# Local attention with a routed mixture of experts: 16-bit one-hot tables, slot lines by rounding, gate columns in one load, and a new order of work

## The chip, the cores and the metric

The kernel runs on one core of one Trainium2 chip. The metric is the device time of one execution in microseconds (us); the figure before the change is the median of three runs. An execution that was recorded by the hardware profiler gives the page and the rows below.

## What is computed

Causal attention in a window of 128 positions with a linear bias for each head (8 batches, 8 heads, 576 positions, 64 wide), and behind it a mixture of 8 experts with the two best for each of the 4608 tokens:

```python
scores = np.where(mask, scale * q @ k.T + bias, -1e9)       # 0 <= i - j < 128
x = (softmax(scores) @ v)  ->  (4608, 512)
noisy = x @ w_gate + np.log1p(np.exp(x @ w_noise)) * noise
top2 = the two largest of the 8 noisy logits; top2_w = softmax over the two
for e in range(8):
    h = np.maximum(x[mask_e] @ w1[e], 0.0)                  # 512 -> 1024
    out[mask_e] += top2_w * (h @ w2[e])                     # 1024 -> 512
```

## The kernel before, in words

**The order is made while the program is built.** Each piece of work is a strand, a Python generator that asks for an engine with a planned cost in us and a due time (its rank), for a buffer of a ring, or for an event. The class `Order` simulates the engines by those costs: each free engine takes the ready piece with the lowest rank, and in that order the instructions are written into each engine's queue. On the chip the queues are then worked off in that fixed order, each instruction waiting for its data. So a planned cost never changes an instruction, only the order. The constants at the top (`ZERO` to `LARGEST`) are offsets of due times and delays; `STAGE` has one for each step of an attention unit, `FFN0, FFN1` spread the due times of the first wave's products, `HOLD` holds the first two experts' weight loads until a planned time, `PACE` and `REST` space the later ones. `Order.cost` raised each VectorE cost by 3% once the planned time was past `FFN1`.

**Attention** goes in 32 pairs of heads (4 for each batch) by 5 units of 128 positions. A unit's scores are made on TensorE (`scores`, line 598), VectorE adds the bias and takes the row extremes (`top`, 604), ScalarE takes the exponential (`soft`, 612), TensorE turns it (`trans`, 619), ScalarE or VectorE copies it back (`evac`, 305), and `weigh` (636) multiplies with the values. The values carry 16 further columns with the products of values and gate weights, so that the same `weigh` brings the gate logits: `gates_of_values` multiplies the transposed values `vt` by `wgn` (525). `wgn` holds w_gate and w_noise at two column offsets, zero elsewhere; four loads fill it (`gate_weight`, 447) over a memset. All direct loads are issued by SyncE, in its own fixed order.

**Routing** of a batch (`route`) makes the noisy logits, the two best experts and each token's slot in its expert's list. A slot number is split into a line and a column of 64 (`halves`): by a shift and a mask on integers, with copies between types. Then two one-hot tables are made by comparing with a running number, for 10 = 5 x 2 (tile, choice) entries each: `hot[0]` by 80 (expert and line, 893) and `hot[1]` by 64 (column, 897). The second is multiplied by the token numbers (901, on GpSimd in six batches, on VectorE in two), and ten matmuls (`list_`, 905) sum the entries into 80 lines of 64, which GpSimd adds into the lists in memory. `next_lines` makes the lines from which the next batch goes on.

**The experts** run in two waves. The first takes experts 0 and 1 with the tokens that early batches gave (blocks of 256, 256, 256, 192), during attention and behind it: gathers, splitting of tokens and weights into two 16-bit parts, up products (1459), ReLU (1618, 1650), down products (1659), scatters that add into the output (1796). The second takes what is left of these and the six other experts, ranked by the length of their lists; their blocks of 512 tokens use a seven-product scheme (1496) whose sums of tokens, weights and quadrants are made on VectorE (1274, 1574 to 1611). VectorE also makes the low parts of the weights (1270, 1290) and of the tokens (1399). Expert 2's loads (1192) need the ranking, which needs the last batch's routing.

Of the kernel before, what the change touches and what calls it, by code (L numbers as in the profile page):

```python
# [29 lines left out]
LINE, SPAN = 64, 10  # L30
LINES = 88
# [16 lines left out]
ZERO = 2019.65  # L48
LOAD = 1075.19
VALUES = 1169.98  # L50
GATE = (413.12, 503.1)
GATES = -311.61
ROUTE = -79.16
SCATTER = (-1036.89, -486.7, 213.65)
FFN0, FFN1 = 288.77, 555.18
WEIGHTS = ((918.12, 272.55), (959.66, -236.26))
SEQUENCE = ((0, 0), (0, 1), (1, 0), (1, 1), (0, 2), (1, 2), (0, 3), (1, 3))
TOKENS = -394.6
STAGE = (538.41, 414.48, -338.92, -406.83, 42.73, -373.27, 193.47, -830.41)
# [60 lines left out]
class Order:  # L120
# [141 lines left out]
def attention_moe(ctx: ExitStack, tc: tile.TileContext, qk_, v, vt_, w_gate, w_noise, noise, w12,  # L262
# [83 lines left out]
    steps_ = const.tile([128, E * SPAN], F16, name="steps")  # L346
    numbers = const.tile([128, NQ], F32, name="numbers")
# [8 lines left out]
    lines_ = const.tile([128, 2, E], I32, name="lines")  # L356
# [31 lines left out]
    def set_ups():  # L388
# [9 lines left out]
        def counts_():  # L398
            for t, pattern, first_, step in ((steps_, [[1, E * SPAN]], 0, 0), (numbers, [[64, NQ]], 1, 1),
# [37 lines left out]
    def gate_weights():  # L437
        yield begun
        parts = Event(4)
        for z, w in enumerate((w_gate, w_noise)):  # L440
            for h in range(2):
                spawn(gate_weight(z, w, h, parts))
        yield parts
        mark(gated)

    def gate_weight(z, w, h, parts):
        yield from move(2e4, -LOAD + GATES, lambda: nc.sync.dma_start(
            wgn[h * D:h * D + D, :, h * 16 + z * E:h * 16 + z * E + E],
            dram(w, h * D * E, [[E, D], [128 * E, 4], [1, E]])))
        mark(parts)  # L450
# [275 lines left out]
    def divided(k, low, high, r7):  # L726
# [24 lines left out]
        yield dve(0.45, r7, sums)  # L751
        for o, i, c in halves_:
            to = xs_[y][:, i:NQ:2].rearrange("p i (h c) -> p i h c", h=4)[:, :, 2 * z:2 * z + 2]
            lt = lts[b][:, i:NQ:2, 2 * (k % NP):2 * (k % NP) + 2]
            yield dve(0.49 if c == 3 else 0.36, r7, lambda: times(o, i, c, to, 0, D))
            yield dve(0.2 if c == 3 else 0.17, r7, lambda: times(o, i, c, lt, D, D + 16))
# [77 lines left out]
    def route(b):  # L834
# [7 lines left out]
        yield act(0.09, rank, lambda: nc.scalar.activation(u, lg[:, :, 8:16], AF.Abs))  # L842
# [3 lines left out]
        yield act(0.1, rank, lambda: nc.scalar.activation(positive, lg[:, :, 8:16], AF.Relu), False)  # L846
# [42 lines left out]
        def tables(eng, z):  # L889

            if z == 0:
                shape = [128, 2 * NQ, E * SPAN]
                eng.tensor_tensor(hot[0], ef.rearrange("p i k -> p (i k)")[:, :, None].to_broadcast(shape),
                                  steps_[:, None, :].to_broadcast(shape), op=OP.is_equal)
            elif z == 1:
                shape = [128, 2 * NQ, LINE]
                eng.tensor_tensor(hot[1], d.rearrange("p i k -> p (i k)")[:, :, None].to_broadcast(shape),
                                  steps_[:, None, 0:LINE].to_broadcast(shape), op=OP.is_equal)
            else:
                h = hot[1].rearrange("p (i k) c -> p i (k c)", k=2)  # L900
                eng.tensor_tensor(h, h, numbers[:, :, None].to_broadcast([128, NQ, 2 * LINE]), op=OP.mult)
# [1165 lines left out]
```

## Time and profile before

| what | us |
|---|---|
| median of 3 runs | 1023.29 |
| their range | 1021.52 to 1024.88 |
| the profiled execution's own time | 1020.78 |
| its span, first to last instruction | 1018.9 |

The page gives each engine's busy time, a picture of the span in 40 slices, and the chain of work that ended last. In the rows below an engine is named PE (TensorE products), PEld (its weight loads), DVE (VectorE), ACT (ScalarE), POOL (GpSimd) or SPq (SyncE's queue, which issues loads), and L598 is line 598 of the kernel. The clock column (PEclk) is the granted clock of TensorE as a share of the higher of its two levels, 2.4 GHz; the lower is 1.2.

### The profile page before, as it was taken

How to read it: one execution, taken by the hardware profiler on the slowest of the kernel's cores; microseconds unless marked ns; L12 is line 12 of the kernel's file. 1: busy time of each engine (PE TensorE's matmuls, PEld its weight loads, DVE VectorE, ACT ScalarE, POOL GpSimd, SP SyncE). 2: the span in 40 equal slices, each digit the busy share in tenths (PEclk: the TensorE clock that was granted, in tenths of full speed). 3: DMA queues.
4: the chain of work that ended last, by engine and by line, in shares of the span. 5: the costliest groups of instructions: out<-in, count | busy, mean ns of one | idle time of the engine just before them, and what ended most of it. 6: DMA issues, size and time to landing. Idle time of an engine off the chain costs nothing.

```text
span 1018.9 us, 25787 instructions
## 1 busy us (share of the span) xinstructions
PE 979.8 (96%) x9734; PEld 701.8 (69%) x9734; DVE 796.2 (78%) x2733; ACT 564.3 (55%) x1367; POOL 331.0 (32%) x442
## 2 busy tenths in 40 slices
PE   7999999999899999979999999999999999999997
PEld 4776777776666689657668666856767686666774
DVE  6989989798997633987799598959978995998240
ACT  6977678485535424664567555634665655544221
POOL 1079432343834224321324142404331232321013
PEclk9999999999999999999999999999999999999999
DMA  8999999794149455895559474949693676638024
GB/s 315 410 312 318 312 336 328 236 295 73 42 93 243 76 81 90 162 218 134 94 109 217 104 130 91 226 74 171 97 236 59 151 147 166 108 65 127 4 40 52
DMA packets 175534, 166.59 MB, mean 164 GB/s; under 512 B 128928, under 2 KB 139248, under 8 KB 175408
## 3 DMA queue, kind: packets, MB, share of 16 engines
q1 hardware_dynamic: 157888, 125.59, 45.9%
q0 software_dynamic: 17520, 39.34, 21.8%
q8 instruction: 77, 1.26, 0.5%
q14 instruction: 49, 0.40, 0.1%
HBM read 95.11 MB, written 40.91 MB: 133 GB/s over the span
## 4 chain that ended last, share of the span: by engine, by line
PE 79%; DVE 13%; POOL 2%; DMA 2%; issue 2%; ACT 1%; SPq 0%; POOLq 0%; DVEq 0%; ACTq 0%
PE bank L1659 31%; PE bank L1496 18%; PE bank L1459 12%; PE bank L636 5%; PE bank L1664 4%; PE bank L598 3%; PE bank L619 3%; DVE bhl L1611 1%; DVE p L604 1%; DMA qk<-in_qk_dram 1%; DVE side L1599 1%; DVE held L1290 1%; POOL held L1287 1%; DVE x L748 1%; DVE pT L305 1%
## 5 line engine op out<-in xcount | busy, mean ns | idle before, releaser
L1659 PE MATMUL bank<-held,bhh 128*128 128x512 f16 x734 | 218.4, 379 | 2.6 <-ACT bhh L1618 2.6
L1496 PE MATMUL bank<-bx,held 128*128 128x256 f16 x1824 | 210.5, 273 | 6.8 <-ACT side L301 6.3
L1796 POOL DMA_INDIRECT out_dram<-yo,ix x58 | 96.0, 1655 | 338.0 <-ACT yo L301 281.6
L1496 PEld LDWEIGHTS <-held 128*128 128x128 f16 x1824 | 178.7, 98 | 33.2 <-issue 8.2
L1659 PE MATMUL bank<-held,bhl 128*128 128x512 f16 x367 | 139.1, 379 | 1.5 <-DVE bhl L1611 1.5
L1659 PEld LDWEIGHTS <-bhh 128*128 128x128 f16 x784 | 75.8, 98 | 88.9 <-ACT bhh L1618 4.1
L1459 PE MATMUL bank<-ax,held 128*128 128x256 f16 (+6 forms) x1380 | 133.9, 252 | 2.0 <-DVE ahl L1650 1.5
L1459 PEld LDWEIGHTS <-held 128*128 128x128 f16 x1380 | 115.8, 98 | 17.7 <-issue 3.8
L612 ACT ACTIVATE p<-p,nm 128x192 f32<-128x192 f32 (+2 forms) x288 | 103.7, 427 | 22.4 <-DVE nm L604 21.6
L301 ACT ACTIVATE xt<-xg,fit 128x512 f16<-128x512 f32 (+5 forms) x93 | 62.6, 677 | 60.3 <-DVE fit L1366 27.2
L1618 ACT ACTIVATE bhh<-side 128x512 f16<-128x512 f32 x69 | 42.4, 627 | 94.8 <-DVE side L1599 93.2
L604 DVE CUSTOM_DVE_ANT_0 p<-bank,bias 128x192 f32<-128x192 f32 (+2 forms) x288 | 81.8, 327 | 5.5 <-PE bank L598 4.8
L301 ACT ACTIVATE held<-held,wsc 128x512 f16<-128x512 f32 x93 | 63.3, 713 | 28.9 <-DVE held L1274 14.3
L636 PE MATMUL bank<-vraw,pT 64*64 64x81 f32 (+1 forms) x2048 | 76.7, 240 | 1.6 <-DVE pT L305 0.6
L636 PEld LDWEIGHTS bank<-vraw,pT 64*64 64x64 f32 (+1 forms) x2048 | 68.5, 137 | 10.2 <-issue 2.0
L1338 POOL DMA_INDIRECT xg<-xs_dram,ix x48 | 51.8, 1080 | 70.6 <-DVE xt L1399 36.8
L619 PE MATMUL bank<-ident,p 128*128 128x128 f32 x416 | 68.1, 286 | 6.3 <-ACT pT L301 2.8
L1659 PEld LDWEIGHTS <-bhl 128*128 128x128 f16 x392 | 38.3, 98 | 48.9 <-DVE bhl L1611 2.9
L598 PE MATMUL bank<-qk 64*64 64x192 f32 (+2 forms) x1152 | 65.7, 326 | 6.5 <-DMA qk<-in_qk_dram 5.1
L1290 DVE SCALAR_TENSOR_TENSOR held<-held,wsc,held 128x512 f16<-128x512 f32 x96 | 70.9, 767 | 0.0
L1204 ACT ACTIVATE junk<-held 128x512 bf16<-128x512 f32 x104 | 65.1, 626 | 6.2 <-DMA held<-in_w_dram 4.3
L619 PEld LDWEIGHTS bank<-ident,p 128*128 128x128 f32 x416 | 45.7, 142 | 32.3 <-ACT pT L301 7.6
(284 smaller groups left out, 1793.1 us busy)
## 6 DMA issues: line engine op xcount, KB each, us to landing
held<-in_w_dram SPq DMA_DIRECT2D x61, 512.0 KB
qk<-in_qk_dram SPq DMA_DIRECT2D x31, 576.0 KB
vraw<-in_v_dram SPq DMA_DIRECT2D x16, 810.0 KB
out_dram<-xg SPq DMA_DIRECT2D x10, 1024.0 KB
vt<-in_vt_dram SPq DMA_DIRECT2D x16, 576.0 KB
xs_dram<-x SPq DMA_DIRECT2D x16, 320.0 KB
xs_dram<-x SPq DMA_DIRECT2D x16, 256.0 KB
bx<-xt SPq DMA_TRANSPOSE x96
```

The lines of the kernel that those rows point to most:

```text
L301: nc.scalar.activation(o, i, AF.Copy, **kw)
L598: nc.tensor.matmul(s[j % 2][half:half + 64, o:o + c], qk[rows, j * 64:j * 64 + 64], qk[rows, k1 - c:k1], start=True, stop=True)
L604: nc.vector.tensor_tensor_reduce(out=p[:, place(j):place(j) + c], in0=s[z][:, o:o + c], in1=bias4[:, g, z, 192 - c:192], scale=-0.125, sca ...
L612: nc.scalar.activation(pv, pv, AF.Exp, bias=nm[:, z:z + 1], scale=-1.0)
L619: nc.tensor.transpose(t[:, z * 128:z * 128 + 128], p[:, a * 128:a * 128 + 128], ident)
L636: nc.tensor.matmul(o[z * 64:z * 64 + 64, c:c + VC], pt[rows, slot, from_:from_ + 64], t[rows, block, hh], start=(o is first_, z) not in be ...
L1204: nc.scalar.activation(junk, raws_flat(t, z), AF.Abs, accum_out=wam[:, e % 2, z, f:f + 1])
L1290: nc.vector.scalar_tensor_tensor(lo, t, sc, hi, op0=OP.mult, op1=OP.subtract)
L1459: nc.tensor.matmul(t[:, 0:blk.n], wp[:, c], blk.x[:, x + c, 0:blk.n], start=c == 0 and z == 0, stop=c == 3 and z == 2)
L1496: nc.tensor.matmul(t[:, a % 2 * HALF:a % 2 * HALF + HALF], wp, blk.x[:, x], start=first_, stop=False, skip_group_check=True)
L1659: nc.tensor.matmul(blk.y[j][0:r], h[:, cs], wp, start=f == 0 and m == 0, stop=f == 7 and m == 2)
L1796: ins = nc.gpsimd.indirect_dma_start(out=out, out_offset=bass.IndirectOffsetOnAxis(ap=blk.ix[0:r, j:j + 1], axis=0), in_=t[0:r, 0:DM], in_ ...
```

## The change

Four things are done at once. **Tables:** the running numbers become a tile of 80 x 10 in 16 bits, row and column of each entry are kept as 16-bit tiles of 10, and the tables are laid out with the 10 entries innermost; all operands of the comparisons and of the multiplication are then 16 bits wide. The ten matmuls read the tables with a step of 10 elements. **Slot lines:** the line is found by rounding in float (multiply, add, add and subtract a large constant) in place of the integer shift, mask and copies; `next_lines` does the same. **Gate columns:** the host lays w_gate and w_noise out as `wgn` holds them, zeros included; one load brings them, and four loads and a memset go. **Order:** most due times and delays and a number of planned costs are new, and the 3% on VectorE are gone. The diff, cut to its core; in the lines left out other planned costs change (steps of the route, copies and sums of attention), unused tiles go, and the new argument is passed on:

```diff
+WHOLE = 1.5 * 2.0 ** 23
...
-ZERO = 2019.65
-LOAD = 1075.19
-VALUES = 1169.98
-GATE = (413.12, 503.1)
-GATES = -311.61
-ROUTE = -79.16
-SCATTER = (-1036.89, -486.7, 213.65)
-FFN0, FFN1 = 288.77, 555.18
-WEIGHTS = ((918.12, 272.55), (959.66, -236.26))
+ZERO = 568.27
+LOAD = 1726.35
+VALUES = 1490.02
+GATE = (592.42, -177.32)
+GATES = -1005.92
+ROUTE = 212.24
+SCATTER = (-558.63, -1779.44, 819.06)
+FFN0, FFN1 = 985.65, 988.51
+WEIGHTS = ((1110.18, 235.07), (329.5, -55.75))
 SEQUENCE = ((0, 0), (0, 1), (1, 0), (1, 1), (0, 2), (1, 2), (0, 3), (1, 3))
-TOKENS = -394.6
-STAGE = (538.41, 414.48, -338.92, -406.83, 42.73, -373.27, 193.47, -830.41)
-MIDDLE = 1630.44
-RESULT = -868.28
-WEIGHTS_LATE = 1656.15
-SOON = -776.11
-LISTED = (36.01, -1817.29)
-BIG, PARTS = 1971.78, 542.82
+TOKENS = -135.13
+STAGE = (762.91, 398.43, -692.29, -873.25, -99.37, -122.48, 294.62, -1402.25)
+MIDDLE = 1883.34
+RESULT = -838.1
+WEIGHTS_LATE = 1848.02
+SOON = -880.54
+LISTED = (1020.48, -2157.93)
+BIG, PARTS = 905.87, 883.02
 TIGHT = (1, 5, 7)
-LATE = (964.06, -1700.75, 837.67, 233.39, 327.65, -1019.18, -417.1, -852.6, 26.68, -922.38, 2132.47, 749.7, 255.16, 538.12)
+LATE = (763.07, -727.25, 553.92, 182.73, 524.7, -1504.62, -1803.02, -1298.45, 242.27, -202.09, 2609.41, 245.05, 172.46, 1377.03)
...
-REST = -38.3
-PACE = (68.65, -27.38)
-HOLD = (-376.19, 197.8)
-AHEAD = 1022.78
+REST = -113.98
+PACE = (44.6, -12.0)
+HOLD = (24.18, 221.19)
+AHEAD = 776.98
...
-STAY, TURN = -339.23, 0.13
+STAY, TURN = -180.73, 0.13
...
-LARGEST = 470.85
+LARGEST = 2707.67
...
-        elif e == "DVE" and self.now > FFN1:
-            us *= 1.03
...
-    steps_ = const.tile([128, E * SPAN], F16, name="steps")
-    numbers = const.tile([128, NQ], F32, name="numbers")
+    steps_ = ap_.tile([128, E * SPAN, 2 * NQ], F16, name="steps")
+    numbers = const.tile([128, NQ, 2], F16, name="numbers")
...
-            for t, pattern, first_, step in ((steps_, [[1, E * SPAN]], 0, 0), (numbers, [[64, NQ]], 1, 1),
+            for t, pattern, first_, step in ((steps_, [[1, E * SPAN], [0, 2 * NQ]], 0, 0), (numbers, [[64, NQ], [0, 2]], 1, 1),
...
-        parts = Event(4)
-        for z, w in enumerate((w_gate, w_noise)):
-            for h in range(2):
-                spawn(gate_weight(z, w, h, parts))
-        yield parts
+        yield from move(8e4, -LOAD + GATES, lambda: nc.sync.dma_start(wgn, gate_columns))
         mark(gated)
-
-    def gate_weight(z, w, h, parts):
-        yield from move(2e4, -LOAD + GATES, lambda: nc.sync.dma_start(
-            wgn[h * D:h * D + D, :, h * 16 + z * E:h * 16 + z * E + E],
-            dram(w, h * D * E, [[E, D], [128 * E, 4], [1, E]])))
-        mark(parts)
...
-    lo_ = ap_.tile([128, NQ, 2], I32, name="lo")
-    si = ap_.tile([128, NQ, 2], I32, name="si")
-    hot = [ap_.tile([128, 2 * NQ, c], F16, name=f"hot{c}") for c in (E * SPAN, LINE)]
+    ln = ap_.tile([128, NQ, 2], F32, name="ln")
+    si = ap_.tile([128, NQ, 2], F32, name="si")
+    row, col = (ap_.tile([128, 2 * NQ], F16, name=name) for name in ("row", "col"))
+    hot = [ap_.tile([128, c, 2 * NQ], F16, name=f"hot{c}") for c in (E * SPAN, LINE)]
...
+        def whole_lines(o, i):
+            V.tensor_scalar(o, i, 1.0 / LINE, 0.5 / LINE - 0.5, op0=OP.mult, op1=OP.add)
+            V.tensor_scalar(o, o, WHOLE, WHOLE, op0=OP.add, op1=OP.subtract)
+
         def slot_numbers():
-            with nc.allow_low_precision(reason="whole numbers below 2^24"):
-                V.tensor_reduce(si, oh, axis=AX.X, op=OP.add)
+            V.tensor_reduce(si, oh, axis=AX.X, op=OP.add)
 
         def halves():
-            V.tensor_scalar(both_i, si, 6, None, op0=OP.arith_shift_right)
-            V.tensor_scalar(si, si, LINE - 1, None, op0=OP.bitwise_and)
-            V.tensor_copy(d, both_i)
-            V.scalar_tensor_tensor(ef, ef, float(SPAN), d, op0=OP.mult, op1=OP.add)
-            V.tensor_copy(d, si)
+            row_, col_ = (x.rearrange("p (i k) -> p i k", k=2) for x in (row, col))
+            whole_lines(ln, si)
+            V.scalar_tensor_tensor(row_, ef, float(SPAN), ln, op0=OP.mult, op1=OP.add)
+            V.scalar_tensor_tensor(col_, ln, -float(LINE), si, op0=OP.mult, op1=OP.add)
 
         def next_lines():
-            V.tensor_copy(lines_[:, 0], base)
-            V.tensor_scalar(lines_[:, 1], lines_[:, 0], 6, None, op0=OP.arith_shift_right)
-            V.tensor_copy(line, lines_[:, 1])
+            whole_lines(line, base)
             V.scalar_tensor_tensor(rest_of_line, line, -float(LINE), base, op0=OP.mult, op1=OP.add)
...
-            if z == 0:
-                shape = [128, 2 * NQ, E * SPAN]
-                eng.tensor_tensor(hot[0], ef.rearrange("p i k -> p (i k)")[:, :, None].to_broadcast(shape),
-                                  steps_[:, None, :].to_broadcast(shape), op=OP.is_equal)
-            elif z == 1:
-                shape = [128, 2 * NQ, LINE]
-                eng.tensor_tensor(hot[1], d.rearrange("p i k -> p (i k)")[:, :, None].to_broadcast(shape),
-                                  steps_[:, None, 0:LINE].to_broadcast(shape), op=OP.is_equal)
+            if z < 2:
+                shape = list(hot[z].shape)
+                eng.tensor_tensor(hot[z], (row, col)[z][:, None, :].to_broadcast(shape), steps_[:, 0:shape[1]], op=OP.is_equal)
             else:
-                h = hot[1].rearrange("p (i k) c -> p i (k c)", k=2)
-                eng.tensor_tensor(h, h, numbers[:, :, None].to_broadcast([128, NQ, 2 * LINE]), op=OP.mult)
+                eng.tensor_tensor(hot[1], hot[1], numbers.rearrange("p i k -> p (i k)")[:, None, :].to_broadcast([128, LINE, 2 * NQ]),
+                                  op=OP.mult)
 
         def list_(a):
             for z in range(2 * NQ):
-                nc.tensor.matmul(a[0:E * SPAN, 0:LINE], hot[0][:, z], hot[1][:, z], start=z == 0, stop=z == 2 * NQ - 1)
+                nc.tensor.matmul(a[0:E * SPAN, 0:LINE], hot[0][:, :, z], hot[1][:, :, z], start=z == 0, stop=z == 2 * NQ - 1)
...
-            (0.39, best), (0.39, where),
-            (0.08, lambda: V.tensor_add(ef, idx[:, :, 0:2], inval)),
-            (0.15, lambda: V.tensor_tensor(oh, ef[:, :, :, None].to_broadcast([128, NQ, 2, E]),
+            (0.39, best), (0.62, where),
...
-            (0.5, halves)]
-        onward = [(0.3, next_lines), (0.25, next_places)]
+            (0.75, halves)]
+        onward = [(0.5, next_lines), (0.5, next_places)]
...
-        yield dve(0.98, rank, lambda: tables(nc.vector, 0))
-        yield dve(0.8, rank, lambda: tables(nc.vector, 1))
+        yield dve(0.55, rank, lambda: tables(nc.vector, 0))
+        yield dve(0.45, rank, lambda: tables(nc.vector, 1))
...
-            yield dve(0.8, rank, lambda: tables(nc.vector, 2))
+            yield dve(0.45, rank, lambda: tables(nc.vector, 2))
         else:
-            yield Op((("POOL", 1.55, rank), ("DVE", 0.8, rank + LATE[10])), lambda g: tables(engine[g], 2), slows=0.4)
+            yield Op((("POOL", 1.55, rank), ("DVE", 0.45, rank + LATE[10])), lambda g: tables(engine[g], 2), slows=0.4)
...
-        return dve(0.08 + o.shape[-1] * 0.00112, rank, lambda: nc.vector.tensor_tensor(o, a, b, op=op))
+        return dve(0.34, rank, lambda: nc.vector.tensor_tensor(o, a, b, op=op))
...
-        yield dve(1.3, rank, powers)
+        yield dve(1.15, rank, powers)
...
-        yield dve(0.07 + 0.00115 * c, rank, lambda: nc.vector.scalar_tensor_tensor(lo, x, up_, hi, op0=OP.mult, op1=OP.subtract))
+        yield dve(0.13 + 0.00104 * c, rank, lambda: nc.vector.scalar_tensor_tensor(lo, x, up_, hi, op0=OP.mult, op1=OP.subtract))
...
-            us = 3 * (blk.n / 2400 + 0.005)
+            us = 3 * (blk.n / 2400 + 0.0035)
...
-    nc.gpsimd.memset(wgn, 0.0)
...
+    gates = _np.zeros((2, D, NP, 2, 2, E), a["moe_w_gate"].dtype)
+    for z, name in enumerate(("moe_w_gate", "moe_w_noise")):
+        for h in range(2):
+            gates[h, :, :, h, z] = a[name].reshape(NP, 2, D, E)[:, h].transpose(1, 0, 2)
+    gates = gates.reshape(128, NP, 4 * E)
...
-        "in_w_gate_dram": a["moe_w_gate"],
-        "in_w_noise_dram": a["moe_w_noise"],
+        "in_gate_columns_dram": gates,
```

## Rows read from the trace of the kernel before

**Rows 1.** The page: busy time by engine, and the chain's shares by engine

```profile
PE 979.8 (96%) x9734; PEld 701.8 (69%) x9734; DVE 796.2 (78%) x2733; ACT 564.3 (55%) x1367; POOL 331.0 (32%) x442
...
PE 79%; DVE 13%; POOL 2%; DMA 2%; issue 2%; ACT 1%; SPq 0%; POOLq 0%; DVEq 0%; ACTq 0%
```

**Rows 2.** Busy time by stretch; stretch, length, busy (instructions) by engine, PEclk, DMA, GB/s

```profile
0.00:20.00 20.00, 12.89 (x139) 8.39 (x140) 13.31 (x80) 13.36 (x36) 3.39 (x24) 0.91 0.86 288
60.00:130.00 70.00, 64.75 (x1132) 48.83 (x1128) 64.10 (x320) 51.01 (x146) 49.85 (x60) 0.98 0.94 319
220.00:290.00 70.00, 64.70 (x865) 46.90 (x864) 63.85 (x290) 40.73 (x106) 44.57 (x58) 1.00 0.43 74
350.00:410.00 60.00, 60.00 (x587) 51.42 (x586) 24.02 (x89) 21.79 (x56) 20.83 (x23) 1.00 0.54 87
410.00:460.00 50.00, 43.86 (x307) 30.44 (x306) 46.94 (x128) 32.09 (x73) 15.13 (x16) 0.97 0.92 200
550.00:950.00 400.00, 393.99 (x3019) 274.32 (x3017) 332.03 (x822) 216.90 (x462) 111.00 (x120) 1.00 0.67 130
...
1011.50:1018.90 7.40, 0.00 (x0) 0.00 (x0) 0.00 (x0) 0.33 (x1) 1.54 (x2) 0.78 0.38 55
```

**Rows 3.** Instructions on the tables; duration in ns least/median/longest, first and last start

```profile
L893 DVE TENSOR_TENSOR hot<-ef,steps x8: 975/982/1919, 76.7 to 299.8; 128x800 f16<-128x800 f32 x8
L897 DVE TENSOR_TENSOR hot<-d,steps x8: 761/816/973, 78.9 to 301.5; 128x640 f16<-128x640 f32 x8
L901 POOL TENSOR_TENSOR hot<-hot,numbers x6: 1254/1256/1256, 81.3 to 247.3; 128x640 f16<-128x640 f16 x6
```

**Rows 4.** VectorE by shape, then the list's matmuls; busy us, mean ns

```profile
L871 DVE TENSOR_SCALAR lo<-si 128x10 int32<-128x10 int32 x8 | 2.6, 327 | 0.2
...
L874 DVE SCALAR_TENSOR_TENSOR ef<-ef,d 128x10 f32<-128x10 f32 x8 | 1.4, 171 | 0.3
...
L1620 DVE TENSOR_SCALAR bhh<-side 128x512 f16<-128x512 f32 x3 | 1.3, 420 | 0.0
...
L905 PE MATMUL bank<-hot,hot 128*80 128x64 f16 x80 | 4.4, 202 | 0.2 <-POOL hot L901 0.2
```

**Rows 5.** Timeline of the start; start, us, engine, line, operation, idle before it

```profile
5.08 2.34 SPq L447 DMA_DIRECT2D wgn<-in_w_gate_dram  x2
...
7.46 1.53 SPq L447 DMA_DIRECT2D wgn<-in_w_noise_dram  x2
...
9.09 0.58 SPq L495 DMA_DIRECT2D vt<-in_vt_dram  x1
...
14.24 1.48 SPq L1192 DMA_DIRECT2D held<-in_w_dram  x3
...
14.91 0.78 PE L525 MATMUL bank<-vt,wgn 128*32 128x320 f32 x8 [2.05 <-DMA vt<-in_vt_dram]
```

**Rows 6.** The chain in order of time; start, us, what

```profile
266.91 0.69 DVE idx L854 x5
...
354.21 1.31 PE bank L1459 x12
...
448.32 0.33 DVE xg L1274
...
558.20 1.81 DVE bhl L1611 x3
```

**Rows 7.** Timeline: the last scores on TensorE, and expert 2's first loads on SyncE

```profile
276.50 0.87 PE L598 MATMUL bank<-qk 64*64 64x192 f32 x12 [0.58 <-DVE nm L604]
...
314.45 0.97 SPq L1192 DMA_DIRECT2D held<-in_w_dram  x2
```

**Rows 8.** Change of waves: chain, longest gap of TensorE, ten us by windows

```profile
439.32 1.32 DVE held L1270 x2
...
452.75 2.71 PE L1496 MATMUL bank<-bx,held 128*128 128x256 f16 x12 [5.48 <-ACT side L301]
...
450.00:460.00 10.00, 7.25 (x53) 5.85 (x53) 8.11 (x24) 5.60 (x13) 2.24 (x2) 0.83 0.95 203
```

More of the change, by code (lines that the diff above doesn't have):

```diff
@@ L261, in attention_moe @@
 @with_exitstack
-def attention_moe(ctx: ExitStack, tc: tile.TileContext, qk_, v, vt_, w_gate, w_noise, noise, w12,
+def attention_moe(ctx: ExitStack, tc: tile.TileContext, qk_, v, vt_, gate_columns, noise, w12,
                   out, xs, slots, eye):
@@ L355, in attention_moe @@
     line = const.tile([128, E], F32, name="line")
-    lines_ = const.tile([128, 2, E], I32, name="lines")
     tmp = const.tile([128, 2, E], F32, name="tmp")
@@ L749, in times @@
                             den[:, 1, i:NQ:2, :, None].to_broadcast([128, c, 2, c1 - c0]), op=OP.mult)
-        yield dve(0.45, r7, sums)
+        yield dve(0.41, r7, sums)
         for o, i, c in halves_:
@@ L754, in divided @@
             lt = lts[b][:, i:NQ:2, 2 * (k % NP):2 * (k % NP) + 2]
-            yield dve(0.49 if c == 3 else 0.36, r7, lambda: times(o, i, c, to, 0, D))
-            yield dve(0.2 if c == 3 else 0.17, r7, lambda: times(o, i, c, lt, D, D + 16))
+            yield dve(0.48 if c == 3 else 0.34, r7, lambda: times(o, i, c, to, 0, D))
+            yield dve(0.17 if c == 3 else 0.14, r7, lambda: times(o, i, c, lt, D, D + 16))
             put(ob if c == 3 else tb, o)
@@ L841, in route @@
         positive = oh2.rearrange("p i k e -> p (i k e)")[:, 0:NQ * E].rearrange("p (i e) -> p i e", e=E)
-        yield act(0.09, rank, lambda: nc.scalar.activation(u, lg[:, :, 8:16], AF.Abs))
+        yield act(0.18, rank, lambda: nc.scalar.activation(u, lg[:, :, 8:16], AF.Abs))
         yield act(0.13, rank, lambda: nc.scalar.activation(y_, u, AF.Exp, scale=-1.0))
@@ L845, in route @@
         yield act(0.13, rank, lambda: nc.scalar.activation(l, u, AF.Ln), False)
-        yield act(0.1, rank, lambda: nc.scalar.activation(positive, lg[:, :, 8:16], AF.Relu), False)
+        yield act(0.18, rank, lambda: nc.scalar.activation(positive, lg[:, :, 8:16], AF.Relu), False)
         def best():
@@ L913, in whole_numbers @@
             V.tensor_add(listed, listed, t)
-        r5, both_i = rk[:, 0:NQ], lo_
+        r5 = rk[:, 0:NQ]
         G = V if b == B - 1 else nc.gpsimd
         rest = [
-            (0.09, lambda: V.scalar_tensor_tensor(y_, u, 1.0, y_, op0=OP.subtract, op1=OP.subtract)),
+            (0.18, lambda: V.scalar_tensor_tensor(y_, u, 1.0, y_, op0=OP.subtract, op1=OP.subtract)),
             (0.32, lambda: V.reciprocal(u, u)),
@@ L927, in route @@
         choose = [
-            (0.39, best), (0.39, where),
-            (0.08, lambda: V.tensor_add(ef, idx[:, :, 0:2], inval)),
-            (0.15, lambda: V.tensor_tensor(oh, ef[:, :, :, None].to_broadcast([128, NQ, 2, E]),
+            (0.39, best), (0.62, where),
+            (0.13, lambda: V.tensor_add(ef, idx[:, :, 0:2], inval)),
+            (0.25, lambda: V.tensor_tensor(oh, ef[:, :, :, None].to_broadcast([128, NQ, 2, E]),
                                            iota8[:, None, None, :].to_broadcast([128, NQ, 2, E]), op=OP.is_equal)),
@@ L978, in route @@
         end = yield pe(0.2, rank, ranks, False)
-        yield act(0.1, rank, lambda: nc.scalar.activation(d[:, :, 0], d[:, :, 0], AF.Exp))
+        yield act(0.2, rank, lambda: nc.scalar.activation(d[:, :, 0], d[:, :, 0], AF.Exp))
         yield end
@@ L990, in route @@
         spawn(gates_out(b, rank))
-        yield dve(0.98, rank, lambda: tables(nc.vector, 0))
-        yield dve(0.8, rank, lambda: tables(nc.vector, 1))
+        yield dve(0.55, rank, lambda: tables(nc.vector, 0))
+        yield dve(0.45, rank, lambda: tables(nc.vector, 1))
         if b == B - 1:
-            yield dve(0.8, rank, lambda: tables(nc.vector, 2))
+            yield dve(0.45, rank, lambda: tables(nc.vector, 2))
         else:
-            yield Op((("POOL", 1.55, rank), ("DVE", 0.8, rank + LATE[10])), lambda g: tables(engine[g], 2), slows=0.4)
+            yield Op((("POOL", 1.55, rank), ("DVE", 0.45, rank + LATE[10])), lambda g: tables(engine[g], 2), slows=0.4)
         a = yield (tb, rank)
         yield pe(0.4, rank, lambda: list_(a))
-        yield dve(0.3, rank, lambda: whole_numbers(a))
+        yield dve(0.35, rank, lambda: whole_numbers(a))
         put(tb, a)
@@ L1394, in piece @@
     def piece(blk, j, q, x, up_, rank, done, lows=None):
-        c = x.shape[-1]
+        c = HALF if lows is None and q == 3 else DM
         xt = yield (xtr, rank)
@@ L1691, in downs_of @@
                 for c in range(4):
-                    end = yield pe(3 * (blk.n / 2400 + 0.005), rank, lambda: mm2_flipped(blk, f, c, ev[2]), False)
+                    end = yield pe(3 * (blk.n / 2400 + 0.0035), rank, lambda: mm2_flipped(blk, f, c, ev[2]), False)
                     if f == 7:
```

## The prediction

> **What bounds the kernel now.** I read the page's busy shares and chain first [rows 1]. TensorE is busy for 979.8 of 1018.9 us and carries 79% of the chain that ended last; VectorE carries 13%. No engine but TensorE can be worth more than its gaps: 1018.9 - 979.8 = 39.1 us. The windows then say where they lie [rows 2]: 7.1 us in the first 20, 5.3 from 60 to 130, 5.3 from 220 to 290, 6.1 from 410 to 460, 6.0 in the 400 us from 550 to 950, and 7.4 at the very end, after the last matmul. These make 37.2; the rest is crumbs. The last 7.4 us (a scatter landing and the empty overflow loop) are touched by nothing in the change. So some 30 us can move, and the sum below deals in parts of that. VectorE is the engine that is late at the gaps: 64.1 of 70, 63.9 of 70 and 46.9 of 50 us busy in the three inner stretches, while from 350 to 410 it works 24.0 of 60 with TensorE full. There the kernel has VectorE time that it doesn't use, 50 us before it lacks it.
>
> **The change part by part.**
>
> **One-hot tables.** Per batch VectorE makes a table of 800 and one of 640 elements, 982 and 816 ns [rows 3]. Their difference is 166 ns for 160 elements: 1.04 ns each and 0.15 us fixed. No row has a two-operand instruction with all operands in 16 bits, so I bound it: at worst it stays at 1.04. At best it goes at the rate of the nearest row, a 512-element copy that reads and writes in 420 ns [rows 4]: (420 - 150) / 512 = 0.53 ns, which makes 0.57 and 0.49 us. I take that end: the copy, too, is an elementwise pass between tiles in SBUF with a 16-bit result. That saves 0.41 + 0.33 = 0.74 us a batch, 5.9 us over 8, and 0.33 more in each of the two batches whose multiplication runs on VectorE: 6.6. The Trainium skill, VectorE: DVE Perf Modes, section "Mode 2×_1P — pack two bf16 into one 32-bit read", asks for 16-bit operands with step 1 and 4-byte alignment; the new layout (10 values, 20 bytes, innermost) meets that where the old float operand, broadcast innermost, did not; no run shown here has such an instruction. GpSimd's multiplication (1256 ns [rows 3]) keeps its size: nothing taken.
>
> **Slot lines by rounding.** Five small steps (shift, mask, two copies, one fused) become four without integer types. They take from 171 to 327 ns [rows 4], the upper one a mean with a stretched case in it. Four at 171 are 0.68, five at 171 are 0.86: at least 0.17 us saved, at most about 0.5; I take 0.3, 2.4 us over 8 batches. The next batch's lines lose one of four steps: 0.17 x 7 = 1.2. In all 6.6 + 2.4 + 1.2 = 10.2 us less on VectorE before 305 us. It is not on the end's path as a sum: the 70 us from 60 to 130 hold 5.3 us of TensorE gaps, of which three batches' share (3.8 us of VectorE time) can reach at most 3.8. I take -1.5 us; bounds -4 and +1 (fresh order, a stretched step).
>
> **The list's matmuls.** They read both tables with a step of 20 bytes now, where they read unbroken rows: ten pairs a batch, 80 in all, 202 ns each and overlapped, so that they keep TensorE busy for 4.4 us [rows 4], 0.55 for ten. No row shows a 16-bit operand with a step. From below: nothing. From above I let each row of ten take twice its time: 4.4 us, in attention and so on the path. I take 0, since nothing in the rows speaks for a loss.
>
> **The gate columns.** Four loads hold SyncE's queue for 2.34 + 1.53 = 3.87 us, and behind them wait the first transposed values, issued at 9.09 us; TensorE stands 2.05 us for these until 14.91 [rows 5]. One load with a whole row for each partition takes one issue, 0.6 us by the 0.58 of the row that follows: the values are issued some 3.2 us earlier. The order also holds the first expert's weights until 24 us, which now start at 14.24 [rows 5]. What is late next: the scores behind the gate products need VectorE's row maxima. So I take -1.5 of 2.05; bounds 0 and -3.7 (a clock drop of 1.7 us less as well, as below). GpSimd fills 800 step values where it filled 80: by its 1256 ns for 640 elements [rows 3] at most 1.6 us, ahead of its zeros, for which no TensorE gap of the start waits: nothing; uncovered, 1.6.
>
> **The order.** Every due time is new, and the costs are nearer to the rows: row positions 0.39 to 0.62 us against 0.69 measured, the differences 0.37 to 0.34 against 0.33, 12 products 1.340 to 1.322 against 1.31 [rows 6]. And VectorE's 3% after the first wave is dropped: three steps planned at 0.60 took 1.81 [rows 6], so without the 3% the plan is true. By the due times the first wave's products (from 289-555 to 986-989) stand behind the scores (538-696 to 763-921) now, where they stood before them. Attention then ends sooner, with the last scores now at 276.5 us, and after it come the rank of experts and the loads of expert 2, at 314.45 [rows 7]. Its preparation is what the 410-460 gap waits for: VectorE in a row, and 5.48 us of TensorE at once [rows 8]. VectorE has 36 idle us from 350 to 410 [rows 2]. That gap costs 6.1 us, and 1.7 more: in 450-460 the granted clock is 0.83, the higher level but for 3.4 us at half of it [rows 8]. If all goes, -7.8; if the new order is as late at another place, 0; if it is worse, +4. I take half, -3.5: the first expert's buffers must still be given back first. From 220 to 290 I take -0.5 of 5.3, since GpSimd's weight splitting is not made cheaper. From 550 to 950 I take 0: 6.0 us of gaps in 400 leave little to win.
>
> **Sum.** -1.5 - 1.5 - 3.5 - 0.5 = -7.0 us. The profiled execution took 1020.78 us (span 1018.9 and 1.9 around it): 1013.8. The median of the runs shown, 1023.29, lies 2.5 above the profiled one, so 1023.3 - 7.0 = **1016.3 us** is forecast.
>
> **Rivals.**
> **Slower: no margin in the second wave.** With the 3% gone the plan packs VectorE tightly, and a wait in the trace that the plan doesn't know (GpSimd holding up a VectorE step: the 800-element table has a longest of 1919 ns against 982 [rows 3]) is no longer absorbed. Price: VectorE is busy 332 us from 550 to 950 [rows 2]; 3% is 10.0 us, all of it on TensorE if VectorE ends each block last. With -3 from the start and attention that is +7, 1030 us. It decides once VectorE is above some 95% of each block's time; now it is 83% of the whole stretch. For it: the gaps there already wait for it; against: 1.81 for three steps. 22%.
> **A gap that moves.** Attention's early end makes the weights ready, but TensorE lacks filler during attention: the first wave's products now come later, and the gaps from 60 to 290 grow by what 410 to 460 loses. The tables' gain goes there too, and the start's -1.5 alone remains: 1021.8, between 1020.2 and 1026. 14%.
> **Steps on the list's matmuls.** +4.4 on TensorE, in attention, where it is the bound: 1016.3 + 4.4 = 1020.7. The Trainium skill, SBUF — State Buffer, section "Door 1: The DMA port swizzle (why `[64,N]` ≈ `[32,N]`)", says that each access that leaves a 16-byte line pays, and a step of 20 bytes leaves one every time; no run shown here has this. 4%.
> **The tables don't get faster.** The all-16-bit form stays at 1.04 ns; 3.6 of 10.2 us remain, attention loses 1 us of its gain: 1017.3. It is faster still. 3%.
> The forecast's own case: 57%, from 1007 to 1020.
>
> **How the numbers follow.** A measurement of this kernel tells about 0.3% (3.1 us) from no change: faster is below 1020.2, slower above 1026.4. Faster: 57 + 3 = 60%. Same: 14 + 4 = 18%. Slower: 22%. For 8 in 10 the range goes from 1007 (start -3.7, attention -4, boundary -7.8 together give 1007.8) to 1028, which leaves out the upper half of the slower case (11%) and some 6% below.
>
> **What would show it.** The table rows at 0.57 and 0.49 us (right) or near 0.98; the list's pairs at 0.55 us for ten, or 1.1; one gate issue and the first gate product before 13 us; last scores before 265 us and expert 2's loads before 305; TensorE's gap at the change of waves below 3 us; VectorE between 95 and 100% busy in whole blocks after 550, with TensorE gaps summing above 10 us, would be the slower rival. The forecast is wrong if the gaps inside 20-460 sum to as much as now (17 us) in other places.

## The result, and the profile after

The changed kernel takes 1011.68 us (1010.26 to 1012.88, 4 runs) beside 1022.62 for the kernel before in the same comparison: a ratio of 0.9867, with a 95% interval from 0.9833 to 0.9901. In a second comparison it took 1011.44 beside 1019.47, 0.9909 (0.9888 to 0.9930). So the gain is 8 to 11 us. The forecast was 1016.3, 7.0 below the median it stood on. One of the seven executions of the kernel `order_alone` below took 2551.79 us, and its ratio leaves that one out.

The page of the changed kernel, whose span is 1010.2 us: busy time, and the chain's shares, as in [rows 1].

```profile
PE 983.5 (97%) x9734; PEld 710.2 (70%) x9734; DVE 789.8 (78%) x2727; ACT 560.0 (55%) x1350; POOL 328.4 (33%) x437
...
PE 80%; DVE 11%; POOL 3%; DMA 2%; issue 2%; ACT 1%; SPq 0%; another core or an unknown queue 0%; POOLq 0%; ACTq 0%; DVEq 0%
```

TensorE's gaps fell from 39.1 to 1010.2 - 983.5 = 26.7 us, 12.4 less. But its busy time rose by 3.7, with the same 9734 products. Only the difference, 8.7, reached the span. So there are two things to find: where the gaps went, and what made TensorE's work longer. The same stretches as in [rows 2], with the last one moved to the new end:

```profile
0.00:20.00 20.00, 15.41 (x169) 10.34 (x169) 16.28 (x87) 14.53 (x41) 5.82 (x23) 1.00 0.86 313
60.00:130.00 70.00, 66.25 (x1128) 50.16 (x1130) 60.72 (x314) 53.44 (x153) 47.53 (x60) 0.98 0.89 304
220.00:290.00 70.00, 66.48 (x849) 50.06 (x848) 58.94 (x253) 42.25 (x115) 38.66 (x54) 1.00 0.57 141
350.00:410.00 60.00, 59.44 (x571) 49.96 (x570) 29.43 (x100) 22.18 (x58) 21.75 (x24) 1.00 0.47 86
410.00:460.00 50.00, 47.09 (x339) 32.48 (x337) 48.39 (x132) 30.86 (x70) 19.45 (x16) 1.00 0.95 186
550.00:950.00 400.00, 398.87 (x3066) 279.19 (x3064) 333.40 (x815) 218.99 (x457) 108.02 (x120) 1.00 0.63 128
1002.80:1010.20 7.40, 0.00 (x0) 0.00 (x0) 0.00 (x0) 0.46 (x1) 1.54 (x2) 0.82 0.35 53
```

Read the second number against the length. The gaps are now 4.6 us in the first 20 (7.1 before), 3.8 from 60 to 130 (5.3), 3.5 from 220 to 290 (5.3), 2.9 from 410 to 460 (6.1), and 1.1 in the 400 us from 550 to 950 (6.0). The end is the same 7.4. VectorE works 29.4 us from 350 to 410 where it worked 24.0. The granted clock is 1.00 in the first 20 us, where it was 0.91, and 1.00 from 410 to 460, where it was 0.97. The second of these does not hold in every execution. In a second profile of the changed kernel, from the second comparison, the gap there is 2.8 us and the clock is at 0.97 again:

```profile
410.00:460.00 50.00, 47.16 (x334) 33.03 (x333) 47.48 (x125) 30.99 (x70) 15.54 (x15) 0.97 1.06 192
```

What made TensorE's work longer stands in the rows of the tables, to be read beside [rows 3] and [rows 4] (durations least/median/longest; the last three lines are groups by shape with their busy us and mean ns: the list's matmuls and their weight loads, then the weight loads of the kernel before):

```profile
L889 PE MATMUL bank<-hot,hot x80: 277/320/324, 83.8 to 313.9; 128*80 128x64 f16 x80
L882 DVE TENSOR_TENSOR hot<-row,steps x8: 515/567/570, 75.0 to 309.7; 128x800 f16<-128x800 f16 x8
L882 DVE TENSOR_TENSOR hot<-col,steps x8: 478/486/1043, 75.8 to 310.9; 128x640 f16<-128x640 f16 x8
L884 POOL TENSOR_TENSOR hot<-hot,numbers x6: 1312/1317/1324, 77.3 to 242.6; 128x640 f16<-128x640 f16 x6
...
L889 PE MATMUL bank<-hot,hot 128*80 128x64 f16 x80 | 12.4, 317 | 0.0
L889 PEld LDWEIGHTS <-hot 128*80 128x80 f16 x80 | 11.9, 233 | 0.1
L905 PEld LDWEIGHTS <-hot 128*80 128x80 f16 x80 | 4.1, 121 | 1.1 <-ACT pT L301 0.3 <-DVE ahl L1650 0.3
```

VectorE's two comparisons went from 982 and 816 to 567 and 486 ns. The 80 list matmuls that read those tables with a step of 20 bytes keep TensorE busy for 12.4 us where they took 4.4: 8.0 more, on the engine that bounds the kernel. The rise of 3.7 is then 8.0 for the list, less 4.3 on other products. The clock is not shown to be the cause of these 4.3: its mean rose from 0.993 to 0.997 in this profile, but only to 0.995 in the second one, whose busy time is no higher (983.2 us). Their cause stays open.

### The profile page after: what moved, and what is told of

It reads as the page before. It is cut to its first block, busy times and chain, and to the rows that moved or that the text cites. A ratio compares the mean times of both kernels' runs of the same rounds, so it can differ in the third digit from the quotient of the medians.

```text
span 1010.2 us, 25806 instructions
## 1 busy us (share of the span) xinstructions
PE 983.5 (97%) x9734; PEld 710.2 (70%) x9734; DVE 789.8 (78%) x2727; ACT 560.0 (55%) x1350; POOL 328.4 (33%) x437
## 4 chain that ended last, share of the span: by engine, by line
PE 80%; DVE 11%; POOL 3%; DMA 2%; issue 2%; ACT 1%; SPq 0%; another core or an unknown queue 0%; POOLq 0%; ACTq 0%; DVEq 0%
PE bank L1643 28%; PE bank L1480 19%; PE bank L1443 10%; PE bank L624 6%; PE bank L586 4%; PE bank L1648 4%; PE bank L607 4%; DVE held L1274 2%; POOL held L1271 1%; PE bank L889 1%; DVE xt L1383 1%; PE bank L513 1%; DMA held<-in_w_dram 1%; DMA bx<-xt 1%; DVE held L1258 1%
## 5 line engine op out<-in xcount | busy, mean ns | idle before, releaser
L300 ACT ACTIVATE xt<-xg,fit 128x512 f16<-128x512 f32 (+4 forms) x98 | 65.4, 675 | 57.0 <-DVE fit L1350 27.2
L300 ACT ACTIVATE held<-held,wsc 128x512 f16<-128x512 f32 x89 | 60.8, 714 | 50.2 <-DVE held L1258 26.6
L1602 ACT ACTIVATE ahh<-bank 128x256 f16<-128x256 f32 (+1 forms) x63 | 23.2, 369 | 82.0 <-PE bank L1643 39.6
```

The source lines that it names most:

```text
L300: nc.scalar.activation(o, i, AF.Copy, **kw)
L1602: nc.scalar.activation(o, i, AF.Relu)
```

## The experiments

Two theories stood against each other: the new order carries the gain, or the edits (VectorE's saved time, the gate load) do. Beside them was the question of what the list's step costs on the path. Every ratio is to runs of the kernel before in the same comparison, whose median was 1020.63, 1019.47 or 1019.97.

### Old instructions in the new order, and the reverse

In a planned order the emitted instructions and their sequence can be parted: a strand's planned costs and due times are taken from one kernel, what it emits from the other. In the first kernel below the integer slot lines, the float tables and the four loads of before are emitted in the changed sequence; TensorE's and ScalarE's sequences are the same as the changed kernel's, instruction by instruction. The second is the reverse.

```diff
 # order_alone: the kernel before, with
-ZERO = 2019.65  ...  LARGEST = 470.85
+ZERO = 568.27   ...  LARGEST = 2707.67
 # and every planned cost as in the changed kernel
 # edits_alone: the changed kernel, with the constants and costs of before
```

> The instructions of the kernel before (float tables, integer slot lines, four gate loads) in the order of the changed one, engine by engine. Theory 1, the order carries the gain and the list's matmuls take some 8 us of it back (80 of them keep TensorE busy for 12.4 us in the changed kernel, 4.4 before): 1004 to 1009 us, because the 8 us come back and VectorE's some 10 us more are partly covered. Theory 2, VectorE's saved time and the gate load carry the gain: 1018 us or more.

> The changed kernel's instructions (16-bit tables, rounded lines, one gate load) in the order of the kernel before. Theory 1 (order carries the gain, the list's step costs TensorE 8 us): 1024 to 1031 us, no faster than before. Theory 2 (the edits carry it): 1012 to 1017 us.

Measured: the order alone 1015.20 us, ratio 0.9934 (0.9907 to 0.9960); the edits alone 1021.11, ratio 1.0016 (0.9997 to 1.0035). Each theory was half wrong. The order gains, but 1015 is not the 1004 to 1009 that it should have been without the list's 8 us. The edits alone change nothing that can be measured. Together they seem to gain more than the sum: 0.9867 and 0.9909 against 0.9934 x 1.0016 = 0.9950, though with intervals of 0.002 to 0.003 to either side the second of these is at the edge of the noise. Windows of the order alone, stretches 0-20, 60-130, 410-460, 550-950:

```profile
0.00:20.00 20.00, 12.69 (x138) 8.43 (x140) 13.43 (x80) 13.80 (x38) 3.39 (x24) 0.91 0.85 278
60.00:130.00 70.00, 64.28 (x1112) 48.04 (x1105) 63.36 (x312) 53.07 (x149) 46.76 (x56) 0.95 0.89 302
...
410.00:460.00 50.00, 44.34 (x302) 29.60 (x300) 44.73 (x118) 27.84 (x62) 15.89 (x15) 0.93 1.05 179
...
550.00:950.00 400.00, 398.95 (x3087) 280.96 (x3085) 333.48 (x816) 219.75 (x460) 107.70 (x120) 1.00 0.66 131
```

and of the edits alone:

```profile
0.00:20.00 20.00, 14.80 (x169) 10.07 (x169) 16.38 (x87) 14.62 (x41) 5.96 (x24) 1.00 0.85 315
60.00:130.00 70.00, 66.84 (x1193) 50.87 (x1189) 61.13 (x323) 51.84 (x150) 48.84 (x63) 1.00 0.96 329
...
410.00:460.00 50.00, 43.86 (x303) 30.35 (x301) 46.25 (x127) 31.70 (x73) 15.24 (x16) 0.93 0.92 201
...
550.00:950.00 400.00, 394.01 (x3020) 274.42 (x3019) 332.01 (x823) 217.13 (x463) 111.47 (x120) 1.00 0.67 131
```

Set beside [rows 2] and the changed kernel this settles one place and bears on three others. The second wave's gaps (6.0 to 1.1 us) are the order's: 1.1 with it, 6.0 without.

At the start the gaps (7.1 to 4.6) go with the edits: 5.2 with them, 7.3 without, and so does the clock (1.00 against 0.91). But a gap is not the same as lost time, since products that last longer fill it. The kernel before and the edits alone have the same sequence on TensorE, so the same products can be set side by side, first before, then with the edits:

```profile
9.21 1.10 PE L598 MATMUL bank<-qk 64*64 64x64 f32 x24 [0.54 <-DMA qk<-in_qk_dram]
15.62 1.99 PE L598 MATMUL bank<-qk 64*64 64x64 f32 x24
18.98 0.87 PE L598 MATMUL bank<-qk 64*64 64x192 f32 x12
```

```profile
9.34 1.99 PE L588 MATMUL bank<-qk 64*64 64x64 f32 x24 [0.82 <-DVE pT L306]
15.40 1.10 PE L588 MATMUL bank<-qk 64*64 64x64 f32 x24
17.24 0.87 PE L588 MATMUL bank<-qk 64*64 64x192 f32 x12
```

With the edits one group of 24 short scores takes 1.99 us in place of 1.10, although the clock's column says 1.00 there, and the next such group takes 1.10 in place of 1.99. By the last twelve scores the edits are 1.7 us ahead (18.98 to 17.24). That is what the start gains, and it lies behind the first gate product, where the clock no longer falls.

From 60 to 130 the gaps go with the edits as well: 3.2 against 5.7. The change of waves has its small gap only with both: 5.7 with the order, 6.1 with the edits, 2.9 with both. The two large ones differ, though. With the edits alone TensorE stands 5.48 us for ScalarE's `side`, as in [rows 8]. With the order alone that wait is gone, and two others, for what ReLU leaves in the first wave (`ahh`, `ahl`), make up most of the gap:

```profile
446.20 1.03 PE L1657 MATMUL bank<-held,ahh 128*128 128x512 f16 x2 [2.08 <-ACT ahh L1616]
...
450.28 0.61 PE L1657 MATMUL bank<-held,ahl 128*128 128x512 f16 x1 [3.04 <-DVE ahl L1648]
```

So the order alone got the list's 8 us back and lost more than that in gaps: 1013.9 - 977.7 = 36.2 us of them in its profile, 9.5 more than in the changed kernel. Its sequence was planned on table costs of 0.55 and 0.45 us and emitted with tables of 0.98 and 0.82; that this is the reason is likely, but not shown.

### The list's step

```diff
-hot = [ap_.tile([128, c, 2 * NQ], F16, ...) for c in (E * SPAN, LINE)]
+hot = [ap_.tile([128, NQ, c, 2], F16, ...) for c in (E * SPAN, LINE)]
...
-    nc.tensor.matmul(..., hot[0][:, :, z], hot[1][:, :, z], ...)
+    nc.tensor.matmul(..., hot[0][:, z // 2, :, z % 2], hot[1][:, z // 2, :, z % 2], ...)
```

with `row`, `col`, the running numbers (80 x 2 in place of 80 x 10) and the multiplication adapted; the sequence is the changed kernel's.

> The changed kernel with the tables laid out by tile, column and pair of choices (2 innermost, not 10), so that the list's matmuls step by 4 bytes and not by 20; same order. If the step is what makes them slow: ten of them back from 1.55 us to between 0.55 and 0.8, and 1004 to 1007 us if all of it is on the path, while the 800-element table stays near 567 ns. Rival: with 2 innermost VectorE falls back to 982 ns for it, and 1005 to 1010. Rival: the list's matmuls are covered by gaps of attention: 1010 to 1012.

Measured: 1004.02 us, ratio 0.9849 (0.9820 to 0.9878). That is 7.4 to 7.7 us under the changed kernel's two medians, which come from other comparisons, and 7.5 under the changed kernel with four gate loads (below), which ran beside it and took 1011.48. The tables of this kernel, the list by shape, and a stretch of its windows:

```profile
L889 PE MATMUL bank<-hot,hot x80: 192/203/261, 82.3 to 306.4; 128*80 128x64 f16 x80
L882 DVE TENSOR_TENSOR hot<-row,steps x8: 511/564/567, 74.9 to 303.1; 128x800 f16<-128x800 f16 x8
...
L889 PE MATMUL bank<-hot,hot 128*80 128x64 f16 x80 | 4.6, 207 | 0.0
...
60.00:130.00 70.00, 64.62 (x1180) 48.73 (x1181) 61.72 (x336) 55.12 (x157) 48.08 (x61) 1.00 0.93 313
```

The matmuls are back at 203 ns and 4.6 us, and VectorE's 800-element comparison stays at 564: with a pair innermost it loses nothing. The step was the cause, and its 7.8 us lay on the path almost whole: the sequence is the same, the first of the list's matmuls starts 1.5 us earlier (83.8 to 82.3) and the last 7.5 us earlier (313.9 to 306.4). From 60 to 130 the gap is 5.4 us, larger than the changed kernel's 3.8, and yet 1180 products are made in place of 1128: the slow list had filled that gap. In the order of the kernel before:

> The changed instructions with the list's step at 4 bytes, in the order of the kernel before. Theory: the edits were worth some 8 us there too, and the list's step took them: 8 us below the edits in that order, 1011 to 1014, that is 7 to 9 under the kernel before. Rival: without the new order VectorE's saved time is not used: 1016 to 1020.

Measured: 1015.74 us, ratio 0.9962 (0.9946 to 0.9977); the edits with the long step were at 1.0016. That is 5.4 of 8 us. It is 1.7 us above the range that I expected and 0.3 below the rival's; against the kernel before it is 4.2 us, where I expected 7 to 9. The rows of the list's matmuls show it on the way, for the kernel before, the edits alone, and the edits with pairs, all in the old order:

```profile
L905 PE MATMUL bank<-hot,hot x80: 189/203/223, 85.3 to 304.7; 128*80 128x64 f16 x80
L891 PE MATMUL bank<-hot,hot x80: 275/320/392, 82.1 to 304.2; 128*80 128x64 f16 x80
L891 PE MATMUL bank<-hot,hot x80: 192/203/226, 81.8 to 298.3; 128*80 128x64 f16 x80
```

At the first list matmul the edits are 3.2 us ahead, at the last 0.5; with pairs they are 3.5 and then 6.4 us ahead. So the edits are worth 4 us in the old order, and the step took them all. VectorE's saved time is used there only in part, which lies between the theory and the rival.

### The gate load

The four loads and the memset are put back into the changed kernel, everything else in the same sequence.

> The changed kernel with four gate loads and the memset in place of one load, in the same order. If SyncE's issue time held up the first values: first gate product 1.5 to 3 us later than 14.8 us, TensorE's gap there back at 1 to 3 us, 1012.5 to 1015 us. Rival: the bytes ahead of the values set their landing: no later product, 1011 to 1012 us.

Measured: 1011.48 us, ratio 0.9922 (0.9894 to 0.9951). The changed kernel took 1011.68 and 1011.44 in the other comparisons, at ratios whose intervals overlap with this one: no difference clear of the noise. SyncE's issues and the first gate product, first with four loads, then in the changed kernel; the last row is the first gate product of `order_alone`, which has the same four loads in the same sequence:

```profile
4.86 2.81 SPq L445 DMA_DIRECT2D wgn<-in_w_gate_dram  x2
7.71 1.42 SPq L445 DMA_DIRECT2D wgn<-in_w_noise_dram  x2
9.17 0.73 SPq L493 DMA_DIRECT2D vt<-in_vt_dram  x1
...
15.36 0.75 PE L523 MATMUL bank<-vt,wgn 128*32 128x320 f32 x8 [0.68 <-ACT p L610]
```

```profile
4.85 0.78 SPq L437 DMA_DIRECT2D wgn<-in_gate_columns_dram  x1
5.68 1.40 SPq L483 DMA_DIRECT2D vt<-in_vt_dram  x1
...
14.82 0.74 PE L513 MATMUL bank<-vt,wgn 128*32 128x320 f32 x8
```

```profile
15.10 0.75 PE L523 MATMUL bank<-vt,wgn 128*32 128x320 f32 x8 [1.83 <-DMA vt<-in_vt_dram]
```

The values are issued 3.5 us earlier with one load, and the first product comes 0.5 us earlier, not 1.5 to 3: the theory falls, and the time is the rival's. In either kernel TensorE no longer waits for the values (2.05 us before, [rows 5]). The single load is not what ended that wait: with four loads it is gone too, while `order_alone` still has 1.83 us of it. What differs is the work in front: one group of 24 short scores takes 1.99 us in the two kernels here and 1.10 in `order_alone`. Why it lasts longer was not tested. So the load is worth some 0.5 us at the start, and nothing that can be measured in the whole.

### Which part of the order

The changed kernel itself ran beside three others: with the 3% on VectorE's planned costs from 555 us on; with all planned costs of before and the new due times; with the due times of before and the new costs.

```diff
 # three_percent
+        elif e == "DVE" and self.now > 555.18:
+            us *= 1.03
```

> The changed kernel itself, beside the others on one chip. 9 to 12 us below the kernel before; the base for the three others.

> The changed kernel with the 3% on VectorE's planned costs back, from the planned time 555 us on as before (the changed constants would start it at 988); the order differs from planned mid-span on. Theory: the true costs are what closed the second wave's gaps (6.0 us to 1.1 from 550 to 950): the gaps there return, 3 us or more, and 1014 to 1018 us. Rival, of the prediction: the margin helped, and the gaps shrink or stay at 1.1: 1009 to 1012.

> The changed kernel's instructions and due times, planned with all the costs of the kernel before (3% too, from 988 us planned). Theory: due times and costs belong together, and with wrong costs the gaps of attention and of the change of waves grow: 1014 to 1022 us. Rival: the due times carry the order's gain alone: 1010 to 1013.

> The changed kernel's instructions and planned costs, with the due times and delays of the kernel before. Theory: without the new due times the gain of the order is lost, and the list's step stays: 1019 to 1028 us. Rival: the costs carry the order's gain: 1010 to 1014.

Measured: the changed kernel 1011.44 (0.9909); with the 3% 1009.51, ratio 0.9905 (0.9888 to 0.9921); with old costs 1015.54, 0.9959 (0.9945 to 0.9973); with old due times 1059.26, 1.0387 (1.0354 to 1.0420). The 3% are worth nothing that these runs can tell, which refutes my theory here and the prediction's rival too: from 550 to 950 the gaps are 0.6 us with them. With the costs of before, the new due times are still worth 0.6% (0.9959 against 1.0016 for the edits in the old order, two comparisons), and the new costs bring 4 us more. The second wave's gaps go with the due times: with old costs they are 0.9 us. Old due times with the new costs came out far worse than the 1019 to 1028 that I expected: TensorE's busy time from 220 to 290 and 460 to 550:

```profile
220.00:290.00 70.00, 59.01 (x682) 42.89 (x681) 45.38 (x226) 32.05 (x86) 29.30 (x40) 0.83 0.37 87
...
460.00:550.00 90.00, 81.71 (x552) 54.39 (x551) 75.00 (x191) 45.10 (x98) 26.05 (x26) 0.98 0.82 155
```

The gaps are 11.0 and 8.3 us, and the clock of the first stretch is 0.83.

### Two single due times

```diff
 # first_wave_ahead (two other uses of FFN1 kept at their values)
-FFN0, FFN1 = 985.65, 988.51
+FFN0, FFN1 = 288.77, 555.18
 # no_hold
-HOLD = (24.18, 221.19)
+HOLD = (-376.19, 221.19)
```

> The changed kernel with one due time put back: the first wave's products from 289 to 555 (ahead of the scores) in place of 986 to 989 (behind them); nothing else. Theory of the prediction: attention then ends some 20 us later (last scores at 270 or more, not 256), expert 2's loads come later, and the gap at the change of waves grows: 1014 to 1020 us. Rival: expert 2's loads hang on GpSimd and the last routing, not on the scores: loads within 5 us of 320, gap from 410 to 460 as it is, 1010 to 1013 us.

> The changed kernel without holding the first expert's weight loads until 24 us (as before; they start in the first 15 us again). If these loads took the start's bandwidth: TensorE's gaps in the first 60 us grow from some 6.5 by 1 to 3 us, 1012 to 1015. Rival: nothing waits for it: 1009 to 1012, or a fresh order's scatter of some us either way.

Measured: 1035.83 us, ratio 1.0170 (1.0138 to 1.0202), for the first wave ahead of the scores; 1020.77, 1.0010 (0.9996 to 1.0024), without the hold. Both cost far more than expected. The last scores and expert 2's loads in the changed kernel, then the same two in the first kernel, with one of its windows:

```profile
255.50 0.87 PE L586 MATMUL bank<-qk 64*64 64x192 f32 x12
...
320.61 3.30 SPq L1176 DMA_DIRECT2D held<-in_w_dram  x6
```

```profile
293.10 0.87 PE L586 MATMUL bank<-qk 64*64 64x192 f32 x12
...
331.84 2.85 SPq L1176 DMA_DIRECT2D held<-in_w_dram  x5
...
220.00:290.00 70.00, 59.55 (x769) 43.96 (x768) 57.32 (x260) 40.77 (x115) 40.99 (x52) 0.93 0.50 139
```

Attention does end 38 us later when the first wave goes ahead, and the loads 11 us later; the gap at the change of waves grows to 10.0 us and moves behind 460. So the direction holds. But as much is lost from 220 to 290, where the gaps are 10.5 us against 3.5 and the clock is at 0.93. The hold at the start, which I took for a matter of the first 60 us, costs 9 us when it is left out. Nothing of that is lost in the first 20 us: the gaps are 7.2 us there against 4.6 (or 5.3 in the second profile of the changed kernel), but 169 products are made in each, and the same twelve scores start at 17.55 and 17.66. The gaps that grew lie further on, as from 60 to 130 (6.0 against 3.8) and from 220 to 290 (5.6 against 3.5). A single constant reorders all that follows it. How much of the 24 and 9 us is the named mechanism and how much a plan out of joint stays open.

### Both small gains

> The paired tables in the order planned with 3% on VectorE: if both small gains add, 1001 to 1004 us; if the 3% were noise, 1003 to 1006, as with the pairs alone.

Measured: 1003.14 us, ratio 0.9829 (0.9806 to 0.9852): the time of the pairs alone within the noise (0.9849), and the lowest median of this study. It lies in both expected ranges, so it does not decide whether the 3% add anything; the paired tables are the improvement.

## Why the prediction was right, point by point

**Right in sign and range, by terms that partly cancelled.** 7.0 us were forecast, 8 to 11 came. That the total came so close is luck.

**The bound** was read rightly: the gaps of TensorE moved, the last 7.4 us did not. The three inner gaps, which the prediction summed to 17 us, make 10.2, so the rival of a gap that moves did not come. A rise of TensorE's busy time was in it only as a rival of 4%.

**One-hot tables:** 0.57 and 0.49 us were taken, 567 and 486 ns measured. The rule of the Trainium skill that was weighed beside it (VectorE: DVE Perf Modes, "Mode 2×_1P — pack two bf16 into one 32-bit read") is borne out by these rows. Slot lines: 0.3 us a batch were taken; the five steps of before took 1.19 us (mean durations summed), the four of after 0.84. In all VectorE lost 8.7 us in the profile with the old order (796.2 to 787.5), 10.2 were taken. The term on the path, -1.5, has the size by which the gap from 60 to 130 shrank (5.3 to 3.8), but that is chance, since the slow list filled part of that stretch. In the old order with pairs the edits are 2.0 us ahead at 20 us in TensorE's sequence and 5.0 at 130, so that the term was worth some 3, within its bound of -4. **From 220 to 290** -0.5 was taken and the gap shrank by 1.8; with the order alone it is 4.5 us and with the edits alone 4.6, so both had a part.

**The list's matmuls:** the step that failed. I took 0 with an upper bound of 4.4; it was 8.0 in the profile and 7.4 in time. The doubling was an arbitrary bound: no row had a step, so twice the busy time was a guess where the weight load had to be counted too. It went from 121 to 233 ns, and the list kept TensorE busy for 155 ns a pair (12.4 / 80) where it had been 55. The rival that named this had the effect and too small a price; it also got 4% where it was simply true. The Trainium skill, SBUF — State Buffer, section "Door 1: The DMA port swizzle (why `[64,N]` ≈ `[32,N]`)", says that each access that leaves a 16-byte line pays. These runs agree: 20 bytes paid, 4 bytes did not; no step between was tried.

**The gate columns:** -1.5 was taken, and at the start the edits gain 1.7 us (18.98 to 17.24). The size was right, the reason was not. The sign named for it, a first product before 13 us, did not come (14.82): the values are issued earlier, but the products in front take longer, and the gate product comes only 0.1 us earlier than in [rows 5]. What is won lies behind it, in the fall of the clock that the prediction had only in its bound; the load by itself gives some 0.5. GpSimd's 800 step values took 2.69 us where 80 had taken 0.21, 2.5 more and not at most 1.6.

**The order:** at the change of waves -3.5 was taken; the gap lost 3.2 us. The clock's 1.7 us are not reliably won: one profile of the changed kernel has 1.00 there, the other 0.97. The reason was half right: the scores end at 256 and not 277, but expert 2's loads come at 320.61, later than the 314.45 of [rows 7] and not before 305. Between them stands GpSimd, as the chain of the changed kernel shows:

```profile
261.71 1.58 POOL held L1271
...
263.37 1.43 POOL held L1272
...
267.43 1.54 POOL held L1271
```

It splits expert 1's weights in the middle of the last batches' routing. Earlier loads are then not what closed the gap. What the runs show is that VectorE works ahead: 29.4 against 24.0 us from 350 to 410, 35.0 with the pairs. Its work on weights (`held`) is 5.2 us there against 1.5 before. The order alone has 5.5 and is rid of the wait of 5.48 us; the edits alone have 1.5 and keep it. Which piece of that work decides was not tested.

**The second wave** was the other mis-sized term: 0 was taken where the order brought 4.9 us (6.0 to 1.1). I reasoned that 6.0 us of gaps in 400 leave little to win; nearly all of them went. The rival that the margin's loss would cost 10 us there fell: the gaps are at 1.1 without the 3% and at 0.6 with them.

Of the two errors, +8.0 and -4.9 us, the second takes back part of the first, and the 4.3 us by which its other products kept TensorE less busy, which the sum did not have and whose cause stays open, take back the rest. That is why the total was close.

## What to carry to other kernels

When a layout is changed for one engine, price its readers on every other engine: here VectorE's 0.74 us a batch was paid for with 1.0 us a batch of the engine that bounds the kernel, and a layout with two elements innermost serves both. A planned order is fitted to its costs: the edits gave nothing measurable and the order 0.7% apart, 0.9 to 1.3% together, and old due times with new costs lost 4%. Sum TensorE's busy time and its gaps apart, because a gain in one can hide a loss in the other. And do not take a smaller gap for time won: where the sequence is the same, compare when the same product starts.

## What the hardware showed that was not expected

Where both 16-bit operands of a product have a step of 20 bytes, both instructions of TensorE last longer: the matmul 320 ns and not 203, the weight load 233 and not 121, ten pairs 1.55 us and not 0.55. Which of the two reads sets this was not parted. A step of 4 bytes costs nothing that shows (203 ns). VectorE's comparison with all operands in 16 bits goes at 0.51 ns an element ((567 - 486) / 160), against 1.04 with a float operand, and this holds with only two elements innermost and one operand repeated over the middle: 564 ns for 800 elements, where ten innermost take 567. GpSimd's multiplication of the same 640 elements took 1317 ns with ten innermost and 1257 with two. The clock's column does not show everything at the start: it says 1.00 for the first 20 us of the edits alone, while the same form of 24 scores takes 1.99 us at 9.34 and 1.10 us at 15.40.
